# A sparse-attention and two-MoE kernel: later transposes of folded logits, ranks in portions, some local masks added by VectorE, last rows in separate tiles

## The chip, the core and the metric

The kernel runs on one core of a Trainium2 chip. A core has five engines with queues of their own, which meet only at semaphores: TensorE (PE, matrix products into PSUM; its weight loads are listed as PEld), VectorE (DVE), ScalarE (ACT), GpSimd (POOL) and SyncE (SP, which issues transfers). The metric is the device time of one execution in microseconds (us).

## The reference

```python
scores = scale * np.matmul(q, k.transpose(0, 1, 3, 2))          # batch 4, heads 8, seq 576, head_dim 64
mask_local = (rel >= 0) & (rel < 32)                            # heads 0 to 3
mask_strided = (rel >= 0) & (k_pos % 32 == q_pos % 32)          # heads 4 to 7
attn = softmax(np.where(masks, scores, -1e9)); x = attn @ v     # 2304 tokens x 512
h = np.maximum(x @ w_in, 0.0)                                   # d_ff 2048
x2 = (s * h * h + b) @ w_out
logits = x2 @ w_gate                                            # 8 experts
# all (token, expert) pairs by falling logit; a pair is taken if the token is free
# and the expert has fewer than 288 tokens
out[mask_e] = np.maximum(x2[mask_e] @ w1[e], 0.0) @ w2[e]       # per expert, F 1024
```

All data are fp32. The weights of the first layer pair come as 64-bit words, and the kernel converts them on chip.

## The kernel before, in words

**Products.** A matrix product in fp32 is made of three fp32r products: each operand is split into a rounded part and a rest (`xh`/`xl`, `wh`/`wl`, `u[:, 0]`/`u[:, 1]`), the rounded part by ScalarE, the rest by a subtraction on VectorE (L331, L350, L631).

**Stages.** Attention is cut into 32 units (`attn_unit`: a batch b, a pair of heads hp, a half hf). A unit writes a mask into PSUM by a bf16 matmul with the identity (L232), adds the scores of its blocks onto it (L239), and then VectorE takes the row maxima (L244), subtracts (L259), ScalarE takes the exponential, VectorE sums and scales (L264 to L267), PE transposes (L273) and multiplies with v (L294). Units with hp 0 and 1 are local: five blocks of 96 keys (hf 0, 480 columns) or four (hf 1, 384 columns). In batches 0 and 1 (b below `SEG` = 2) the exponential reads PSUM directly; batches 2 and 3 run between the matmuls of the hidden layer.

The tokens then go in six groups g of 384. `h_step(g, fc)` makes one of 16 slices of the hidden layer: twelve matmuls (L441), squared ReLU on ScalarE (L446, L447), and the slice goes to DRAM (`ud`). The logits come from the slices folded with `w_out @ w_gate` (L479): for groups 4 and 5 at once (`h_step`), for groups 0 to 3 (`DG`) later from DRAM (`fold_late`). `logits(g)` copies the folded sums from PSUM (ScalarE, L503), transposes them (PE, L507), reduces (VectorE, L512, L513), and when groups 0 to 3, or 4 and 5, are all there, `ranks` compares each expert pair of a token: seven steps of three operations (L525 to L527).

**The late layer.** x2 itself is made late: `late_step(g, fc)` loads a hidden slice back, splits it (L628 ScalarE, L631 VectorE) and queues nine matmuls (L658). `x2_late` hands them out one by one; they fill PE while other engines do the routing. `x2_row` (L496) scales a row tile and SyncE writes it to DRAM (`x2d`).

**Routing.** `route` runs seven rounds; a round finds each expert's threshold by four counts over 64 candidates (VectorE comparisons, PE sums L787 and L790), then a prefix over tokens (L694 to L700). At the end a last prefix, index arithmetic on VectorE (L798 to L825) and L830 make the list of tokens per expert (L834). Each yield of `route` carries a number of late matmuls to be put in.

**Experts.** `first_gather` fetches the first expert's rows by indirect transfers (GpSimd, L859), PE does the rest of the late layer beside it (L866); then each expert takes two layers (L912, L937). The last expert writes its rows in three parts (`put`, L980 to L982).

**Order.** The order on every engine is the order in which the program emits (`manual_schedule`). `Pipe.tick` advances all live generators by one `yield`; the loop of `mix1` emits, per step, folds (`FT` = 3 ticks), from n = 96 on `LF` = 3 late matmuls, and one tick of the pipe of `h_step`. A `yield` more in `logits` or `ranks` thus moves what follows it behind what others emit in that tick, and the loop ends only when all generators have ended.

Of the kernel before, what the change touches and what calls it, by code (L numbers as in the profile page):

```python
# [8 lines left out]
F32 = mybir.dt.float32  # L9
# [4 lines left out]
ALU = mybir.AluOpType  # L14
AX = mybir.AxisListType
# [47 lines left out]
class Body:  # L63
    B = 4
    H = 8
    S = 576
# [6 lines left out]
    NG = 6  # L73
    E = 8
    CAP = 288
# [62 lines left out]
    def constants(self):  # L138
# [26 lines left out]
        for h in (0, 64):  # L165
            nc.vector.tensor_copy(self.mstr[h:h + 36], t1[h:h + 36, :36].unsqueeze(1).to_broadcast([36, 8, 36]))
        self.Es = [c.tile([128, 8, 64], F32, name=f"E{i}") for i in range(self.NE)]
        for E in self.Es:
            nc.gpsimd.memset(E, 0.0)
        self.onesf = c.tile([128, 128], F32, name="onesf")  # L170
# [50 lines left out]
    def attn_unit(self, b, hp, hf):  # L221
        nc = self.nc
        loc = hp < 2
        p, nb, kw = (64, 5 - hf, 96) if loc else (36, 8, 36)
        pr = 64 + p
        qk, vs = self.load_unit(b, hp, hf)
        for _ in range(self.LOADLAG):
            yield
        sp = self.ps()
        m = self.mloc[:, hf:] if loc else self.mstr  # L230
        w = nb * kw
        nc.tensor.matmul(sp[:, :w], self.identb, m.rearrange("p c k -> p (c k)"),  # L232
                         start=True, stop=False, skip_group_check=True)
        for c in range(nb):
            q0 = c * p + 32 if loc and hf else c * p
            k0 = max(0, q0 - 32) if loc else q0
            for j in range(2):
                sl = slice(64 * j, 64 * j + 64)
                nc.tensor.matmul(sp[64 * j:64 * j + p, c * kw:(c + 1) * kw], qk[sl, 0, q0:q0 + p],  # L239
                                 qk[sl, 1, k0:k0 + kw], start=False, stop=(c == nb - 1), skip_group_check=True)  # L240
        yield
        nm = self.p2.tile([128, 2, 8], F32, tag="nm", name=self.nm("nm"), bufs=6)
        mx, sm = nm[:pr, 0, :nb], nm[:pr, 1, :nb]
        nc.vector.tensor_reduce(mx, sp[:pr, :w].rearrange("p (c k) -> p c k", c=nb), axis=AX.X, op=ALU.max, negate=True)  # L244
        if loc:
            E = self.wt([128, nb, kw], F32, "E")
        else:
            Ep = self.Es[self.ne % self.NE]
            self.ne += 1
            E = Ep[:, :, :36]  # L250
        if loc and b < self.SEG:
            nc.vector.tensor_scalar(mx, mx, 0.125, None, op0=ALU.mult)
            yield from self.lag(0, b)
            for c in range(nb):
                nc.scalar.activation(E[:pr, c, :], sp[:pr, c * kw:(c + 1) * kw], AF.Exp, bias=mx[:, c:c + 1],
                                     scale=0.125, accum_out=sm[:, c:c + 1])
            yield from self.lag(1, b)
        else:
            nc.vector.tensor_tensor(E[:pr], sp[:pr, :w].rearrange("p (c k) -> p c k", c=nb),  # L259
                                    mx.unsqueeze(2).to_broadcast([pr, nb, kw]), op=ALU.add)  # L260
            yield from self.lag(0, b)
            nc.scalar.activation(E[:pr], E[:pr], AF.Exp, scale=0.125)
            yield from self.lag(1, b)
            nc.vector.tensor_reduce(sm, E[:pr], axis=AX.X, op=ALU.add)  # L264
        nc.vector.tensor_scalar(sm, sm, 1e-9, None, op0=ALU.add)
        nc.vector.reciprocal(sm, sm)
        nc.vector.tensor_tensor(  # L267
            E[:pr], E[:pr], sm.unsqueeze(2).to_broadcast([pr, nb, kw]), op=ALU.mult)
        yield from self.lag(2, b)
        tps = [self.ps() for _ in range(2 if loc else 1)]  # L270
        for c in range(nb if loc else 4):
            if loc:
                nc.tensor.transpose(tps[c % 2][:96, 128 * (c // 2):128 * (c // 2) + 128], E[:, c, :], self.identf)  # L273
            else:
                nc.tensor.transpose(tps[0][:, 128 * c:128 * c + pr], Ep[:pr, 2 * c:2 * c + 2, :].rearrange("p m k -> p (m k)"),
                                    self.identf[:pr, :pr])
        yield
        eTs = []
        for t, tp in enumerate(tps):
            h, kr = ((nb - t + 1) // 2, 96) if loc else (4, 100)  # L280
            src = tp[:kr, :128 * h].rearrange("k (c j i) -> k c j i", j=2, i=64)[:, :, :, :p]
            eT = self.wt([128, h, 2, p], F32, "eT")
            (nc.vector.tensor_copy if (t and b > 1 if loc else self.TV) else nc.scalar.copy)(eT[:kr], src)
            eTs.append(eT)
        yield from self.lag(3, b)
        o = [self.ps() for _ in range(1 if loc else 2)]
        for c in range(nb):
            for j in range(2):
                if loc:
                    out, eT = o[0][64 * j:64 * j + 64, c * p:(c + 1) * p], eTs[c % 2][:96, c // 2, j, :]  # L290
                else:
                    m, k = c % 2, c // 2
                    out, eT = o[m][64 * j:64 * j + 64, k * p:(k + 1) * p], eTs[0][64 * m:64 * m + 36, k, j, :]
                nc.tensor.matmul(out, vs[c][:, j, :], eT, start=True, stop=True, skip_group_check=True)  # L294
        yield
        if b not in self.xb:
            self.xb[b] = self.xf.tile([128, 4, 576], F32, tag="xb", name=self.nm("xb"))
        if loc:
            nc.scalar.copy(self.xb[b][:, hp, 320 * hf:320 * hf + p * nb], o[0][:, :p * nb])
        else:  # L300
            dst = self.xb[b][:, hp, :].rearrange("d (i m c) -> d m c i", m=2, c=8)[:, :, 4 * hf:4 * hf + 4]
            for m in range(2):
                (nc.vector.tensor_copy if m and self.OV else nc.scalar.copy)(
                    dst[:, m], o[m][:, :144].rearrange("d (c i) -> d c i", c=4))
        self.units += 1
# [194 lines left out]
    def logits(self, g, pf):  # L500
        nc = self.nc
        fo = self.wt([128, self.G], F32, "fo")
        nc.scalar.copy(fo, pf[:, :self.G])  # L503
        yield
        ps = self.ps()
        for t in range(3):
            nc.tensor.transpose(ps[:, t * 128:(t + 1) * 128], fo[:, t * 128:(t + 1) * 128], self.identf)  # L507
        yield
        L = self.L[:, 3 * g:3 * g + 3, :]
        for t in range(3):  # L510
            v = ps[:, t * 128:(t + 1) * 128].rearrange("p (j k) -> p k j", j=4)[:, :8, :]
            nc.vector.tensor_reduce(L[:, t, :], v, axis=AX.X, op=ALU.add)  # L512
        nc.vector.scalar_tensor_tensor(L, L, self.sb[:, 0:1], self.lc.unsqueeze(1).to_broadcast([128, 3, 8]),  # L513
                                       op0=ALU.mult, op1=ALU.add)
        self.ranked.add(g)
        for gs in (range(4), range(4, 6)):
            if g in gs and self.ranked.issuperset(gs):
                self.ranks(3 * gs[0], 3 * gs[-1] + 3)

    def ranks(self, i, j):  # L520
        tt = self.nc.vector.tensor_tensor
        L, R = self.L[:, i:j, :], self.R[:, i:j, :]
        for d in range(1, 8):
            ge = self.ge[:, i:j, :8 - d]
            tt(ge, L[:, :, :8 - d], L[:, :, d:], op=ALU.is_ge)  # L525
            tt(R[:, :, :8 - d], R[:, :, :8 - d], ge, op=ALU.add)
            tt(R[:, :, d:], R[:, :, d:], ge, op=ALU.subtract)  # L527

    def mix1(self):
        nc = self.nc  # L530
# [436 lines left out]
    def last_expert(self, e, X, w1, w2):  # L967
        nc = self.nc
# [7 lines left out]
                                 start=(fc == 0 and i == 0), stop=(fc == 7 and i == 2))  # L976

        def put(c):
            t = self.wt([96, 512], F32, "yr")
            nc.scalar.copy(t[:, :256], y[c][:96, :256])  # L980
            nc.vector.tensor_copy(t[:, 256:], y[c][:96, 256:])
            nc.gpsimd.indirect_dma_start(  # L982
                out=self.a["out"][:, :],
                out_offset=bass.IndirectOffsetOnAxis(ap=self.idx[:, 3 * e + c:3 * e + c + 1], axis=0),
                in_=t, in_offset=None)
# [122 lines left out]
```

## Time and profile before

| | us |
|---|---|
| median of 3 runs | 823.06 |
| lowest, highest | 822.31, 823.54 |
| profiled execution | 822.38 |
| its span | 820.3 |
| PE busy (share of the span) | 798.2 (97%) |
| VectorE busy | 473.6 (58%) |
| ScalarE busy | 370.3 (45%) |

The mean granted clock of TensorE is 0.992 of full speed. A busy engine is not an engine at its peak: matmuls overlap, and their ends are modelled; the time from one start to the next is what a matmul costs, and the chain of waits counts so. In an idle entry such as `[2.15 <-DVE u L631]` the number is how long the engine stood still before the row, and behind the arrow is what ended it. A line number is that of the kernel before unless said otherwise.

### The profile page before, as it was taken

How to read it: one execution, taken by the hardware profiler on the slowest of the kernel's cores; microseconds unless marked ns; L12 is line 12 of the kernel's file. 1: busy time of each engine (PE TensorE's matmuls, PEld its weight loads, DVE VectorE, ACT ScalarE, POOL GpSimd, SP SyncE). 2: the span in 40 equal slices, each digit the busy share in tenths (PEclk: the TensorE clock that was granted, in tenths of full speed). 3: DMA queues.
4: the chain of work that ended last, by engine and by line, in shares of the span. 5: the costliest groups of instructions: out<-in, count | busy, mean ns of one | idle time of the engine just before them, and what ended most of it. 6: DMA issues, size and time to landing. Idle time of an engine off the chain costs nothing.

```text
span 820.3 us, 17310 instructions
## 1 busy us (share of the span) xinstructions
PE 798.2 (97%) x6688; PEld 697.9 (85%) x6688; DVE 473.6 (58%) x1160; ACT 370.3 (45%) x889; POOL 52.2 (6%) x69
## 2 busy tenths in 40 slices
PE   7989999999999999989999999999999999999996
PEld 5779988899999678877777777777899999999994
DVE  8798874667452234066676767565265556455620
ACT  3787665656564464422323222222245455445520
POOL 1000000000000000000000000000203112221211
PEclk9979999999999999999999999999999999999999
DMA  7958745746775894442516233332577566656410
GB/s 186 278 172 257 230 134 170 245 162 225 268 243 177 261 305 174 149 159 79 180 54 205 91 100 109 87 126 69 163 241 212 159 194 213 205 167 207 125 30 29
DMA packets 88753, 140.21 MB, mean 171 GB/s; under 512 B 10848, under 2 KB 52576, under 8 KB 88672
## 3 DMA queue, kind: packets, MB, share of 16 engines
q1 hardware_dynamic: 85600, 129.68, 50.2%
q0 software_dynamic: 3072, 9.44, 3.6%
q8 instruction: 52, 0.85, 0.4%
q14 instruction: 29, 0.24, 0.1%
HBM read 106.32 MB, written 32.77 MB: 170 GB/s over the span
## 4 chain that ended last, share of the span: by engine, by line
PE 92%; DVE 4%; ACT 1%; issue 1%; DMA 1%; POOLq 0%; POOL 0%; DVEq 0%; ACTq 0%; SPq 0%
PE b L441 26%; PE b L658 21%; PE b L912 12%; PE b L937 11%; PE b L239 3%; PE b L479 2%; PE b L787 2%; PE b L294 2%; PE b L397 2%; PE b L975 1%; PE b L866 1%; PE b L953 1%; PE b L390 1%; PE b L311 1%; PE b L273 1%
## 5 line engine op out<-in xcount | busy, mean ns | idle before, releaser
L658 PE MATMUL b<-wh,u 128*128 128x512 f32 x544 | 181.7, 404 | 2.6 <-DVE u L631 2.6
L658 PEld LDWEIGHTS b<-wh,u 128*128 128x128 f32 x544 | 101.6, 188 | 23.8 <-DVE u L631 3.8
L628 ACT CAST u<-r 128x384 fp32r<-128x384 f32 (+1 forms) x96 | 47.3, 496 | 161.8 <-PE b L658 127.0
L658 PE MATMUL b<-wl,u 128*128 128x512 f32 x272 | 106.8, 393 | 0.0
L937 PE MATMUL b<-u,wh 128*128 128x288 f32 x448 | 93.5, 302 | 0.0
L446 ACT ACTIVATE r<-b 128x384 f32<-128x384 f32 x96 | 47.1, 491 | 101.7 <-PE b L441 101.6
L441 PE MATMUL b<-xh,wh 128*128 128x384 f32 x384 | 89.9, 355 | 0.0
L350 DVE TENSOR_TENSOR wl<-raw,wh 128x512 fp32r<-128x512 f32 x128 | 82.9, 684 | 0.3
L441 PE MATMUL b<-xl,wh 128*128 128x384 f32 x384 | 83.0, 337 | 0.0
L441 PE MATMUL b<-xh,wl 128*128 128x384 f32 x384 | 82.8, 336 | 0.0
L912 PE MATMUL b<-X,wh 128*128 128x288 f32 x512 | 78.1, 295 | 0.6 <-ACT X L885 0.6
L348 ACT CAST wh<-raw 128x512 fp32r<-128x512 f32 x128 | 73.5, 620 | 4.0 <-DVE u L631 4.0
L441 PEld LDWEIGHTS b<-xh,wh 128*128 128x128 f32 x384 | 64.6, 190 | 12.1 <-issue 10.0
L912 PEld LDWEIGHTS b<-X,wh 128*128 128x128 f32 x512 | 71.5, 188 | 1.4 <-ACT X L885 0.7
L937 PEld LDWEIGHTS b<-u,wh 128*128 128x128 f32 x448 | 71.0, 188 | 0.0
L441 PEld LDWEIGHTS b<-xl,wh 128*128 128x128 f32 x384 | 69.0, 189 | 0.0
L441 PEld LDWEIGHTS b<-xh,wl 128*128 128x128 f32 x384 | 68.5, 189 | 0.0
L919 DVE SCALAR_TENSOR_TENSOR u<-b,u 128x288 fp32r<-128x288 f32 x64 | 29.1, 455 | 66.5 <-ACT u L918 66.5
L937 PE MATMUL b<-u,wl 128*128 128x288 f32 x224 | 65.9, 294 | 0.0
L631 DVE TENSOR_TENSOR u<-r,u 128x384 fp32r<-128x384 f32 (+1 forms) x96 | 48.9, 529 | 21.6 <-ACT u L628 21.6
L658 PEld LDWEIGHTS b<-wl,u 128*128 128x128 f32 x272 | 51.2, 188 | 9.3
L918 ACT ACTIVATE u<-b 128x288 fp32r<-128x288 f32 x64 | 26.4, 412 | 59.3 <-PE b L912 59.3
(201 smaller groups left out, 1164.0 us busy)
## 6 DMA issues: line engine op xcount, KB each, us to landing
raw<-in_moe_w_dram SPq DMA_DIRECT2D x128, 256.0 KB
r<-ud SPq DMA_DIRECT2D x160, 192.0 KB
ud<-r SPq DMA_DIRECT2D x96, 192.0 KB
raw<-in_words_dram SPq DMA_DIRECT2D x64, 256.0 KB
qk<-in_q_dram SPq DMA_DIRECT2D x24, 288.0 KB
x2d<-E SPq DMA_DIRECT2D x18, 256.0 KB
wod<-K SPq DMA_DIRECT2D x16, 256.0 KB
wo<-wod SPq DMA_DIRECT2D x16, 256.0 KB
```

The lines of the kernel that those rows point to most:

```text
L239: nc.tensor.matmul(sp[64 * j:64 * j + p, c * kw:(c + 1) * kw], qk[sl, 0, q0:q0 + p], qk[sl, 1, k0:k0 + kw], start=False, stop=(c == nb - 1 ...
L348: nc.scalar.copy(h, W)
L350: nc.vector.tensor_tensor(l, W, _f(h), op=ALU.subtract)
L441: nc.tensor.matmul(ps[:, :self.G], w[:, dc * 128:(dc + 1) * 128], self.xg[g][dc][x], start=(k == 0), stop=(k == 11))
L446: nc.scalar.activation(r, ps[:, :self.G], AF.Relu)
L628: nc.scalar.copy(d[:, 0, :], src)
L631: nc.vector.tensor_tensor(d[:, 1, :], src, _f(d[:, 0, :]), op=ALU.subtract)
L658: self.nc.tensor.matmul(**args)
L912: self.nc.tensor.matmul(ps[:, :288], w1[dc, fh][wi][:, fs:fs + 128], X[:, xi, dc, :], start=(k == 0), stop=(k == 11))
L918: self.nc.scalar.activation(h, ps[:, :288], AF.Relu)
L919: self.nc.vector.scalar_tensor_tensor(l, ps[:, :288], 0.0, _f(h), op0=ALU.max, op1=ALU.subtract)
L937: nc.tensor.matmul(y[dc][:, :288], w[:, sl], u[:, j, :288], start=(fc == 0 and i == 0), stop=(fc == 7 and i == 2))
```

## The change

1. Local units of batches 2 and 3 put no mask into PSUM. The first score matmul of a block starts it afresh, and VectorE adds the mask (`mloc`) while it copies the scores into E; the maxima and the subtraction then read E.
2. `logits` of groups 0 to 3 yields three times instead of once between the copy and the transposes.
3. `ranks` yields after each of its seven steps.
4. The last expert's rows go into the three tiles `Es`, not into tiles of the common pool.

```diff
--- before.py
+++ after.py
@@ -229,25 +229,31 @@
         sp = self.ps()
         m = self.mloc[:, hf:] if loc else self.mstr
         w = nb * kw
-        nc.tensor.matmul(sp[:, :w], self.identb, m.rearrange("p c k -> p (c k)"),
-                         start=True, stop=False, skip_group_check=True)
+        after = loc and b >= self.SEG
+        if not after:
+            nc.tensor.matmul(sp[:, :w], self.identb, m.rearrange("p c k -> p (c k)"),
+                             start=True, stop=False, skip_group_check=True)
         for c in range(nb):
             q0 = c * p + 32 if loc and hf else c * p
             k0 = max(0, q0 - 32) if loc else q0
             for j in range(2):
                 sl = slice(64 * j, 64 * j + 64)
                 nc.tensor.matmul(sp[64 * j:64 * j + p, c * kw:(c + 1) * kw], qk[sl, 0, q0:q0 + p],
-                                 qk[sl, 1, k0:k0 + kw], start=False, stop=(c == nb - 1), skip_group_check=True)
+                                 qk[sl, 1, k0:k0 + kw], start=after, stop=after or c == nb - 1, skip_group_check=True)
         yield
         nm = self.p2.tile([128, 2, 8], F32, tag="nm", name=self.nm("nm"), bufs=6)
         mx, sm = nm[:pr, 0, :nb], nm[:pr, 1, :nb]
-        nc.vector.tensor_reduce(mx, sp[:pr, :w].rearrange("p (c k) -> p c k", c=nb), axis=AX.X, op=ALU.max, negate=True)
         if loc:
             E = self.wt([128, nb, kw], F32, "E")
         else:
             Ep = self.Es[self.ne % self.NE]
             self.ne += 1
             E = Ep[:, :, :36]
+        S = sp[:pr, :w].rearrange("p (c k) -> p c k", c=nb)
+        if after:
+            nc.vector.tensor_tensor(E, S, m, op=ALU.add)
+            S = E
+        nc.vector.tensor_reduce(mx, S, axis=AX.X, op=ALU.max, negate=True)
         if loc and b < self.SEG:
             nc.vector.tensor_scalar(mx, mx, 0.125, None, op0=ALU.mult)
             yield from self.lag(0, b)
@@ -256,8 +262,7 @@
                                      scale=0.125, accum_out=sm[:, c:c + 1])
             yield from self.lag(1, b)
         else:
-            nc.vector.tensor_tensor(E[:pr], sp[:pr, :w].rearrange("p (c k) -> p c k", c=nb),
-                                    mx.unsqueeze(2).to_broadcast([pr, nb, kw]), op=ALU.add)
+            nc.vector.tensor_tensor(E[:pr], S, mx.unsqueeze(2).to_broadcast([pr, nb, kw]), op=ALU.add)
             yield from self.lag(0, b)
             nc.scalar.activation(E[:pr], E[:pr], AF.Exp, scale=0.125)
             yield from self.lag(1, b)
@@ -501,7 +506,8 @@
         nc = self.nc
         fo = self.wt([128, self.G], F32, "fo")
         nc.scalar.copy(fo, pf[:, :self.G])
-        yield
+        for _ in range(1 if g > 3 else self.FT):
+            yield
         ps = self.ps()
         for t in range(3):
             nc.tensor.transpose(ps[:, t * 128:(t + 1) * 128], fo[:, t * 128:(t + 1) * 128], self.identf)
@@ -515,7 +521,7 @@
         self.ranked.add(g)
         for gs in (range(4), range(4, 6)):
             if g in gs and self.ranked.issuperset(gs):
-                self.ranks(3 * gs[0], 3 * gs[-1] + 3)
+                yield from self.ranks(3 * gs[0], 3 * gs[-1] + 3)
 
     def ranks(self, i, j):
         tt = self.nc.vector.tensor_tensor
@@ -525,6 +531,7 @@
             tt(ge, L[:, :, :8 - d], L[:, :, d:], op=ALU.is_ge)
             tt(R[:, :, :8 - d], R[:, :, :8 - d], ge, op=ALU.add)
             tt(R[:, :, d:], R[:, :, d:], ge, op=ALU.subtract)
+            yield
 
     def mix1(self):
         nc = self.nc
@@ -976,7 +983,7 @@
                                  start=(fc == 0 and i == 0), stop=(fc == 7 and i == 2))
 
         def put(c):
-            t = self.wt([96, 512], F32, "yr")
+            t = self.Es[c].rearrange("p c k -> p (c k)")[:96]
             nc.scalar.copy(t[:, :256], y[c][:96, :256])
             nc.vector.tensor_copy(t[:, 256:], y[c][:96, 256:])
             nc.gpsimd.indirect_dma_start(
```

In the changed kernel line numbers are a few higher: L441 becomes L446, L479 L484, L503 L508, L507 L513, L525 to L527 L531 to L533, L631 L638, L658 L665, L694 L701, L798 L805, L830 L837.

**PE at the logits of group 0.** `b_3268` holds the folded sums, `fo_4127` their copy, `b_4131` (now `b_4158`) the transposes; `xh`, `xl`, `wh` belong to the hidden layer. Before:

```order
L479 MATMUL b_3268<-r_4042,wog 32x384
L479 MATMUL b_3268<-r_4095,wog 32x384
L507 MATMUL b_4131<-identf,fo_4127 128x128 x3
L441 MATMUL b_4153<-xh_3743,wh_1632 128x384
L441 MATMUL b_4153<-xh_3776,wh_1632 128x384
L441 MATMUL b_4153<-xh_3820,wh_1632 128x384
L441 MATMUL b_4153<-xh_3853,wh_1632 128x384
```

In the changed kernel (the four L484 of `b_3268` and the first four L446 of `b_4145` stand right above):

```order
L446 MATMUL b_4145<-xl_3744,wh_1631 128x384
L446 MATMUL b_4145<-xl_3777,wh_1631 128x384
L446 MATMUL b_4145<-xl_3821,wh_1631 128x384
L446 MATMUL b_4145<-xl_3854,wh_1631 128x384
L446 MATMUL b_4145<-xh_3743,wl_1632 128x384
L446 MATMUL b_4145<-xh_3776,wl_1632 128x384
L446 MATMUL b_4145<-xh_3820,wl_1632 128x384
L446 MATMUL b_4145<-xh_3853,wl_1632 128x384
L513 MATMUL b_4158<-identf,fo_4127 128x128 x3
L484 MATMUL b_3317<-r_4097,wog 32x384
L484 MATMUL b_3317<-r_4099,wog 32x384
```

The transposes have moved behind the twelve matmuls of one slice of the hidden layer. For groups 1 and 3 it is the same; for 2, 4 and 5 their place is unchanged.

**VectorE at a local unit of batch 2.** `b_1869` are the scores, `nm` the maxima. Before:

```order
L267 TENSOR_TENSOR E_113<-E_113,nm_1739 100x8x36
L244 TENSOR_REDUCE nm_1946<-b_1869 128x5
L259 TENSOR_TENSOR E_1948<-b_1869,nm_1946 128x480
L283 COPY eT_1971<-b_1935 96x256
L350 TENSOR_TENSOR wl_1904<-K_1726,wh_1903 128x512
```

In the changed kernel:

```order
L272 TENSOR_TENSOR E_113<-E_113,nm_1739 100x8x36
L254 TENSOR_TENSOR E_1946<-b_1869,mloc 128x480
L256 TENSOR_REDUCE nm_1945<-E_1946 128x5
L265 TENSOR_TENSOR E_1946<-E_1946,nm_1945 128x480
L288 COPY eT_1971<-b_1934 96x256
L355 TENSOR_TENSOR wl_1903<-K_1726,wh_1902 128x512
```

One operation more (L254), which reads PSUM; the other two read and write E. On PE the L232 that stood ahead of the L239 of `b_1869` is gone with its weight load: PE has 5481 rows for 5497, VectorE 1125 for 1117.

**VectorE at the ranks of groups 4 and 5.** `ge` and `R` are the comparisons and ranks, `u` the late splits. Before, the end of the 21 operations:

```order
L527 TENSOR_TENSOR R<-R,ge 128x6x2
L525 TENSOR_TENSOR ge<-L 128x6
L526 TENSOR_TENSOR R<-R,ge 128x6
L527 TENSOR_TENSOR R<-R,ge 128x6
L631 TENSOR_TENSOR u_4863<-r_4834,u_4863 128x384
L631 TENSOR_TENSOR u_4908<-r_4842,u_4908 128x384
L631 TENSOR_TENSOR u_4922<-r_4865,u_4922 128x384
L631 TENSOR_TENSOR u_4936<-r_4910,u_4936 128x384
```

In the changed kernel, from the third operation on:

```order
L533 TENSOR_TENSOR R<-R,ge 128x6x7
L638 TENSOR_TENSOR u_4863<-r_4834,u_4863 128x384
L531 TENSOR_TENSOR ge<-L 128x6x6
L532 TENSOR_TENSOR R<-R,ge 128x6x6
L533 TENSOR_TENSOR R<-R,ge 128x6x6
L531 TENSOR_TENSOR ge<-L 128x6x5
L532 TENSOR_TENSOR R<-R,ge 128x6x5
L533 TENSOR_TENSOR R<-R,ge 128x6x5
L531 TENSOR_TENSOR ge<-L 128x6x4
L532 TENSOR_TENSOR R<-R,ge 128x6x4
L533 TENSOR_TENSOR R<-R,ge 128x6x4
L638 TENSOR_TENSOR u_4890<-r_4842,u_4890 128x384
```

The first late split now stands behind three operations, the second behind twelve, the next four behind all 21. On PE 58 matmuls of the late layer instead of 37 stand between the last transposes of logits and the first of the routing, and 28 instead of 49 between L830 and L866.

## Rows read from the trace of the kernel before

**Rows 1.** The profile's page: busy time of each engine, and shares of the chain

```profile
PE 798.2 (97%) x6688; PEld 697.9 (85%) x6688; DVE 473.6 (58%) x1160; ACT 370.3 (45%) x889; POOL 52.2 (6%) x69
...
PE 92%; DVE 4%; ACT 1%; issue 1%; DMA 1%; POOLq 0%; POOL 0%; DVEq 0%; ACTq 0%; SPq 0%
```

**Rows 2.** What PE waited for, whole span (us in total, times, longest)

```profile
PE b L658 <- DVE u L631: 2.6, 3, 2.1
...
PE b L507 <- ACT fo L503: 2.0, 3, 0.7
...
PE b L694 <- DVE rt L766: 0.7, 1, 0.7
PE b L830 <- DVE rt L824: 0.6, 1, 0.6
...
PE b L830 <- DVE rt L825: 0.3, 1, 0.3
```

**Rows 3.** The chain (start us, us, what), 88 to 182 us

```profile
89.15 0.22 PE b L232
...
113.49 0.18 PE b L232
...
166.41 0.16 PE b L232
```

**Rows 4.** VectorE's groups, 88 to 182 us (busy us, mean ns | idle)

```profile
L267 DVE TENSOR_TENSOR E<-E,nm 128x480 f32<-128x480 f32 x4 | 2.6, 658 | 0.1
L259 DVE TENSOR_TENSOR E<-b,nm 128x480 f32<-128x480 f32 x4 | 2.6, 658 | 0.1
...
L331 DVE TENSOR_TENSOR xl<-xb,xh 128x384 fp32r<-128x384 f32 x4 | 2.2, 559 | 6.4 <-ACT xh L330 6.4
L259 DVE TENSOR_TENSOR E<-b,nm 128x384 f32<-128x384 f32 x4 | 2.2, 558 | 0.1
```

**Rows 5.** Busy time by engine, nine stretches from 88 to 182 us together

```profile
sum 94.00, PE 94.00 PEld 84.66 DVE 64.45 ACT 57.53 POOL 0.00; mean PE 10.44 PEld 9.41 DVE 7.16 ACT 6.39 POOL 0.00
```

**Rows 6.** Time line (start us, us, what [idle before <-releaser]), 144 us

```profile
144.65 0.56 DVE L331 TENSOR_TENSOR xl<-xb,xh 128x384 fp32r<-128x384 f32 x1 [0.35 <-ACT xh L330]
...
144.85 0.85 PE L441 MATMUL b<-xl,wh 128*128 128x384 f32 x4
```

**Rows 7.** The chain: logits, one late step, the late matmuls behind the routing

```profile
277.17 0.49 ACT fo L503
...
277.71 0.55 PE b L507 x3
...
300.51 0.33 PE b L507 x3
...
343.20 2.09 PE b L658 x9
...
562.95 11.27 PE b L658 x49
```

**Rows 8.** Time line, VectorE and PE, 348 to 354 us

```profile
348.75 0.20 DVE L525 TENSOR_TENSOR ge<-L 128x42 f32<-128x42 f32 x1
...
352.75 1.96 DVE L631 TENSOR_TENSOR u<-r,u 128x384 fp32r<-128x384 f32 x4
...
353.35 0.73 PE L658 MATMUL b<-wh,u 128*128 128x512 f32 x2 [2.15 <-DVE u L631]
```

**Rows 9.** Time line, VectorE and PE, 549 to 552 us

```profile
550.97 0.43 DVE L631 TENSOR_TENSOR u<-r,u 128x256 fp32r<-128x256 f32 x1 [0.90 <-ACT u L628]
...
551.51 0.16 DVE L798 TENSOR_SCALAR rt<-b 128x8 f32<-128x8 f32 x1
...
549.92 0.23 PE L700 MATMUL b<-gsb,onesb 128*128 128x152 bf16 x1
```

**Rows 10.** Time line of VectorE and GpSimd (POOL), indices and first gather

```profile
562.99 0.18 DVE L834 CAST idx<-b 96x24 int32<-96x24 f32 x1 [1.25 <-PE b L830]
...
578.18 1.08 POOL L859 DMA_INDIRECT xr<-x2d,idx  x1 [372.16 <-PE b L866]
```

## Prediction

> **What bounds the kernel now.** I read the page first. Its first section has TensorE (PE) busy for 97% of the span, VectorE (DVE) for 58%, ScalarE (ACT) for 45%; its fourth gives PE 92% of the chain that ended last, DVE 4%, ACT 1% [rows 1]. The reader is to see that PE sets the time almost throughout, so that an edit is worth what it takes off PE or off a wait of PE. The second view is therefore PE's waits over the whole span [rows 2]: they are few and short, 2.6 us for the split L631, 2.0 us for the folded logits' copy L503, 0.7 us and 0.6 + 0.3 us for routing steps. After that I read, place by place, the chain where the masks and the logits stand [rows 3, 7], VectorE's durations there [rows 4], the engines' busy time [rows 5], and time lines at the places where PE could begin to wait [rows 6, 8 to 10]. The granted clock is no term: in the masks' stretch the row has PE busy for 94.00 of 94.00 us, and the change leaves no new gap there by my forecast [rows 5].
>
> **The change, part by part.** The sum is made against the profiled execution, 822.38 us (span 820.3 and 2.08 around it). The median of the three runs is 823.06, 0.68 above it; I add these 0.68 at the end.
>
> *Masks of batches 2 and 3.* Removed are eight mask matmuls, four of 480 columns and four of 384. On the chain the former are pieces of 0.22 us (four alike), the latter two of 0.18 and two of 0.16 [rows 3]: 4 x 0.22 + 2 x 0.18 + 2 x 0.16 = 1.56 us of PE. A piece runs from start to start, so weight loads that did not hide are in it. The trace has no such addition on VectorE; the nearest row is the subtraction L259 of the same shape, also from PSUM to SBUF, 658 and 558 ns [rows 4]. So VectorE gets 4 x 0.658 + 4 x 0.558 = 4.86 us more. What hides that: in 94 us VectorE is busy 64.45, so nearly 30 us are free [rows 5]. The tight spot is the fifth unit, the first of batch 3: behind its L259 stands the split L331 of token group 2 at 144.65, and PE's first four xl matmuls run from 144.85 in 0.85 us, the last of them on this split [rows 6]. L331 there waited 0.35 us for ScalarE's xh, so an addition of 0.66 in front of it makes it 0.3 us later, of which PE may feel 0 to 0.3. If the cover were gone everywhere, PE would wait 4.86 and gain 1.56: +3.3. Bounds -1.56 to +3.3; I take -1.5, near the chain's pieces, since L331 waits for ScalarE in all four cases here (6.4 us) [rows 4].
>
> The Trainium skill, "TensorE: Matmul & The Clock Gate", section "Back-to-back issue gap", speaks against the size: it gives a sustained spacing of about 131 ns for 512 columns. By that the eight would be worth an estimated 1.0 us, and the sum would be 0.5 us smaller; the pieces of 0.22 us for 480 columns [rows 3] don't agree, and I go by them. "Perfetto Trace Analysis" of the Trainium skill, section "Optimizing Scalar/DVE Operations", gives VectorE about 60 ns of overhead on SBUF and 125 on PSUM; by it the reduction and the subtraction, which now read SBUF, would give back an estimated 16 x 0.065 = 1.0 us of VectorE's time. The trace disagrees: the same shape takes 658 ns from PSUM (L259) and 658 from SBUF (L267) [rows 4], and nothing is given back.
>
> *Transposes of the folded logits.* Before, three times PE ends the fold, waits for the copy L503 and only then transposes: from the copy's start at 277.17 to the end of L507 at 277.71 + 0.55 it is 1.09 us; where the copy had long been done L507 takes 0.33 [rows 7]. That is 0.76 at most each time; the waits themselves add up to 2.0 [rows 2]. The order on PE now has twelve matmuls of a hidden layer between fold and transposes for groups 0, 1 and 3. The copy needs 0.49 us and of those matmuls four take 0.85 [rows 6], twelve over 2; ScalarE's order around it is as before. Bounds 2.0 to 2.3, I take 2.1; it isn't below nothing, since the copy stands where it stood and PE does the same work. Behind it the ranks of groups 0 to 3 come later, but no PE instruction waits for them until the routing.
>
> *Ranks in portions.* At 348.75 VectorE starts 21 small operations, and four late splits L631 stand behind them from 352.75; PE stands still for 2.15 us until 353.35 [rows 8]. PE had run dry 2.15 us earlier, at 351.2. Now a split stands after the first three rank operations, the next after twelve, the others after all 21. Three operations take (352.75 - 348.75) x 3/21 = 0.57 us, so the first split, of 1.96/4 = 0.49 us, ends at about 349.8, 1.4 us ahead of the need. Twelve take 2.29: the second ends at 352.0. A late step is nine matmuls (three row tiles by three products) in 2.09 us [rows 7], so PE needs it at 351.2 + 2.1 = 353.3. The third ends at 348.75 + 4.0 + 3 x 0.49 = 354.2, against 355.4. ScalarE's casts are no limit: the four splits ran without a gap [rows 8]. Gain 2.15; bounds 1.1 (half of it comes back at the second split) and 2.15; it isn't below nothing, since VectorE does the same operations and PE has more to do beside them. The seven extra steps of the loop carry 3 late matmuls each, 21 in all, from behind the routing to in front of it; their sum is the same. Cover given up: behind the routing 28 stay of 49, where 49 take 11.27 us [rows 7], so 21 x 0.23 = 4.8 us less hide the way from the indices to the gathers. The indices are there at 562.99, the first gather starts at 578.18 [rows 10]: 15 us apart, and the gather waits for the last rows of x2, which move along with the late matmuls. Cost 0.
>
> *End of the routing.* The shift by 21 matmuls puts other splits beside the last routing steps. Before, VectorE's L798 stands behind a split at 550.97 that itself waited 0.90 for ScalarE; it starts at 551.51, though PE had its operand by 549.92 + 0.23 [rows 9]; so the L694 behind it waits 0.7, and the L830 0.6 + 0.3 [rows 2]. In the new order the splits ahead of it are of older steps whose casts are done, and I expect L798 straight behind PE. Bounds 0 and 1.6 (all three gone); I take 1.1.
>
> *Last rows in tiles of their own.* The three scatters wait for the same semaphores as before, and each tile is still written by the same copies of ScalarE and VectorE, one behind the other. Worth 0.
>
> Sum: 1.5 + 2.1 + 2.15 + 1.1 = 6.85; 822.38 - 6.85 = 815.5, with 0.68 added 816.2 us.
>
> **The rivals.**
> *New small waits* (R1). The late matmuls now meet other VectorE work than before: a row tile's x2 or a routing step in front of a split. For it: two of the three L658 waits before are of this kind, (2.6 - 2.1)/2 = 0.25 each [rows 2]. Against: they are only two in some 200 us. Ten of them would cost 2.5: 816.2 + 2.5 = 818.7.
> *VectorE's additions come late* (R2). The mask additions stand in front of splits on which the next matmuls rest, at every unit and not only at 144.65; PE then loses 4.86 and gains 1.56. For it: the narrow margin at 144.85 [rows 6]. Against: 30 free us [rows 5]. 816.2 + 4.86 = 821.1.
> *Routing hand-overs* (R3, the other side). Place: the seven routing rounds, each with four counts, four sums of them and a prefix that PE takes over from VectorE, 63 hand-overs. If with the shift the splits, themselves late as at 550.97, stand in front of the routing step at many of them, each costs what L694 waits, 0.7 [rows 2, 9]. It decides from (6.85 + 1.65)/0.7 = 12.1, 13 of the 63 on; with 14 it is 9.8 us: 816.2 + 9.8 = 826.0. For it: the one row of this kind that exists. Against: before it is one of 63.
> *A part does nothing*: the last tiles, as said, by identical waits; that is in the forecast.
>
> **How the numbers follow.** The forecast has 0.68, R1 0.15, R2 0.10, R3 0.07. The forecast's own range: all upper bounds (1.56 + 2.3 + 2.15 + 1.6 = 7.6) give 815.5, 1.0 below for what I don't see: 814.5; the lower ones (1.2 + 2.0 + 1.1 + 0) give 818.8. The range reaches over R1 to 820.0; outside stay R3, most of R2 and a few per cent below. A measurement of this kernel tells 0.2%, 1.65 us, from no change: faster is below 821.4, slower above 824.7. Faster: 0.68 + 0.14 of R1 + 0.05 of R2 = 0.87; same: 0.01 + 0.05 + 0.03 of R3 = 0.09; slower: 0.04.
>
> **What would show it.** In the changed profile's list of PE's waits the row for the logits' copy is gone and that of L631 (now L638) has only the two short ones; L694's and L830's (now L701, L837) shrink. PE has eight mask matmuls fewer, with 1.5 us less PE time between 88 and 182 us and eight new VectorE operations of 0.56 to 0.66. The forecast is wrong in a part if its wait stays or comes back under another name within the next few us: at the first xl matmuls of group 2 for the masks, behind the twelve matmuls for the logits, at the second late step for the ranks, and at the routing's matmuls for the shift.

## The result: 815.11 us, and the profile after

The changed kernel takes 815.11 us (814.41 to 815.69, 4 runs), the kernel before 823.3 in the same comparison (822.31 to 825.18, 4 runs): ratio 0.9898, 95% interval 0.9884 to 0.9912. Two more comparisons gave 0.9903 and 0.9906. The forecast was 816.2. The profiled execution of after took 815.69 (span 813.9), 6.7 less than the one of before; the medians stand 8.2 apart. Why the two differ is the main thing to explain below.

From the page of the changed kernel, busy times and shares of the chain:

```profile
PE 796.1 (98%) x6680; PEld 697.4 (86%) x6680; DVE 477.6 (59%) x1168; ACT 370.3 (45%) x889; POOL 51.8 (6%) x69
...
PE 93%; DVE 4%; ACT 1%; issue 1%; DMA 0%; POOLq 0%; POOL 0%; DVEq 0%
```

PE's share of the chain rose from 92 to 93% [rows 1]; VectorE has 4.0 us more. What PE waited for, whole span (us in total, times, longest):

```profile
...
PE b L299 <- ACT eT L288: 2.1, 3, 1.0
PE b L665 <- DVE u L638: 2.1, 4, 0.8
...
PE b L919 <- ACT X L892: 0.6, 1, 0.6
```

Against [rows 2]: the logits' copy (2.0) is gone, so are the routing's end (0.7, 0.6, 0.3) and the 2.1 us at the ranks. But the late splits (L638 is the L631 of before) still cost 2.1 us, now in four pieces.

**Masks.** Time line of PE at two fixed places, one ahead of the first local unit of batch 2 and one behind the last of batch 3: first in a kernel that has the masks of before (experiment tail_only), then in the changed one.

```profile
81.96 0.30 PE L232 MATMUL b<-mstr,identb 128*128 128x288 bf16 x1
...
271.07 1.02 PE L424 MATMUL b<-acc,onesf 128*128 128x512 f32 x2
```

```profile
83.45 0.30 PE L234 MATMUL b<-mstr,identb 128*128 128x288 bf16 x1
...
271.08 1.02 PE L429 MATMUL b<-acc,onesf 128*128 128x512 f32 x2
```

From mark to mark 189.11 us before, 187.63 after: 1.48 us less, where the sum had 1.5 [rows 3]; the profile of the kernel before has the same 189.11 (83.78 to 272.89). The first mark itself lay between 81.8 and 83.8 us in the profiles of one and the same start, so stages are compared between these two marks, called the first and the second mark below, or from a mark to the end of the span, and not by their place in the span. A part of that spread is the clock: in every profile it falls once more ahead of the first mark, at some 45 to 60 us, in eight of them with 3.4 us lost and in five with 5.1, and the first mark lies at 82.1 us on average in the eight and at 83.0 in the five.

**Logits.** The chain at group 0 (start us, us, what):

```profile
274.43 0.78 PE b L484 x8
275.22 2.31 PE b L446 x12
277.53 0.33 PE b L513 x3
```

The transposes take 0.33 us, as where nothing was waited for [rows 7], and stand right behind the hidden layer's matmuls.

**Ranks.** Time line of VectorE (start us, us, line, operation):

```profile
344.49 0.20 DVE L531 TENSOR_TENSOR ge<-L 128x42 f32<-128x42 f32 x1
...
345.08 0.55 DVE L638 TENSOR_TENSOR u<-r,u 128x384 fp32r<-128x384 f32 x1
...
347.33 0.55 DVE L638 TENSOR_TENSOR u<-r,u 128x384 fp32r<-128x384 f32 x1
...
349.18 1.49 DVE L638 TENSOR_TENSOR u<-r,u 128x384 fp32r<-128x384 f32 x3
```

The first split starts 0.59 us after the first rank operation, the second 2.84 after it, three more in a row behind all 21. PE stood still for 2.15 us at this place [rows 8] and now has no wait. What that is worth from start to start is read from the last transposes of logits to the first prefix of the routing, in the kernel before (the last row is the seventh prefix, of use further on) and in phase_back, which has the same number of late matmuls between the two (time line of PE):

```profile
347.52 0.49 PE L507 MATMUL b<-identf,fo 128*128 128x128 f32 x3
...
386.95 0.24 PE L694 MATMUL b<-rt,ltri 128*128 128x144 bf16 x1
...
549.17 0.24 PE L694 MATMUL b<-rt,ltri 128*128 128x144 bf16 x1
```

```profile
342.44 0.49 PE L513 MATMUL b<-identf,fo 128*128 128x128 f32 x3
...
379.40 0.24 PE L701 MATMUL b<-rt,ltri 128*128 128x144 bf16 x1
```

39.43 us before, 36.96 after: 2.47 less. A listed wait counts from the modelled end of the matmul ahead of it, and this one is 0.3 us shorter than what it cost.

**Routing.** Time line of VectorE, then of PE, in one of the seven rounds:

```profile
412.86 0.17 DVE L805 TENSOR_SCALAR rt<-b 128x8 f32<-128x8 f32 x1 [0.72 <-PE b L707]
...
416.01 1.36 DVE L788 TENSOR_TENSOR rt<-rt,cand 128x1152 bf16<-128x1152 f32 x1
417.28 2.06 DVE L501 SCALAR_TENSOR_TENSOR E<-b,sb,acc 128x512 f32<-128x512 f32 x3
419.26 1.02 DVE L638 TENSOR_TENSOR u<-r,u 128x384 fp32r<-128x384 f32 x2
...
418.64 0.39 PE L665 MATMUL b<-wl,u 128*128 128x512 f32 x1
419.86 0.49 PE L665 MATMUL b<-wh,u 128*128 128x512 f32 x1 [0.83 <-DVE u L638]
```

Here stands a new wait. From 412.86 to 417.37 VectorE makes twelve routing operations up to the comparison L788, then three x2 rows (L501), and only then the split for which PE has waited 0.83 us. The same happens once more 82 us later, and twice without the x2 rows (0.21). From start to start these waits too cost more than is listed; the prefix of the first, second, third and seventh round (from after_third, the changed kernel again):

```profile
384.00 0.24 PE L701 MATMUL b<-rt,ltri 128*128 128x144 bf16 x1
...
410.86 0.24 PE L701 MATMUL b<-rt,ltri 128*128 128x144 bf16 x1
...
438.83 0.24 PE L701 MATMUL b<-rt,ltri 128*128 128x144 bf16 x1
...
548.54 0.24 PE L701 MATMUL b<-rt,ltri 128*128 128x144 bf16 x1
```

A round without such a wait takes 26.86 us, the one with the wait listed at 0.8 takes 27.97: 1.11 more. From the first prefix to the seventh it is 164.54 us here and 162.22 in the kernel before (386.95 to 549.17), so the rounds have become 2.3 us longer. And at the routing's end, VectorE, then PE:

```profile
550.55 0.17 DVE L805 TENSOR_SCALAR rt<-b 128x8 f32<-128x8 f32 x1
...
550.29 0.23 PE L707 MATMUL b<-gsb,onesb 128*128 128x152 bf16 x1
...
553.17 0.24 PE L701 MATMUL b<-rt,ltri 128*128 128x144 bf16 x1
```

L805 starts as soon as L707 is through (550.29 + 0.23), and L701 starts without a wait. Before, the same operation came 1.4 us after PE [rows 9].

### The profile page after: what moved, and what is told of

It reads as the page before. It is cut to its first block, busy times and chain, and to the rows that moved or that the text cites. A ratio compares the mean times of both kernels' runs of the same rounds, so it can differ in the third digit from the quotient of the medians.

```text
span 813.9 us, 17313 instructions
## 1 busy us (share of the span) xinstructions
PE 796.1 (98%) x6680; PEld 697.4 (86%) x6680; DVE 477.6 (59%) x1168; ACT 370.3 (45%) x889; POOL 51.8 (6%) x69
## 4 chain that ended last, share of the span: by engine, by line
PE 93%; DVE 4%; ACT 1%; issue 1%; DMA 0%; POOLq 0%; POOL 0%; DVEq 0%
PE b L446 26%; PE b L665 22%; PE b L919 13%; PE b L944 11%; PE b L241 3%; PE b L794 2%; PE b L484 2%; PE b L299 2%; PE b L402 2%; PE b L982 1%; PE b L873 1%; PE b L960 1%; PE b L395 1%; PE b L316 1%; PE b L278 1%
## 5 line engine op out<-in xcount | busy, mean ns | idle before, releaser
L665 PE MATMUL b<-wh,u 128*128 128x512 f32 x544 | 181.9, 404 | 2.1 <-DVE u L638 2.1
L665 PEld LDWEIGHTS b<-wh,u 128*128 128x128 f32 x544 | 101.5, 188 | 24.0 <-DVE u L638 4.1
L665 PE MATMUL b<-wl,u 128*128 128x512 f32 x272 | 106.8, 393 | 0.0
L446 PE MATMUL b<-xh,wh 128*128 128x384 f32 x384 | 90.0, 356 | 0.0
L446 PE MATMUL b<-xl,wh 128*128 128x384 f32 x384 | 83.0, 337 | 0.0
L446 PE MATMUL b<-xh,wl 128*128 128x384 f32 x384 | 82.6, 336 | 0.0
L919 PE MATMUL b<-X,wh 128*128 128x288 f32 x512 | 78.1, 295 | 0.6 <-ACT X L892 0.6
L446 PEld LDWEIGHTS b<-xh,wh 128*128 128x128 f32 x384 | 64.4, 190 | 13.4 <-issue 11.3
L919 PEld LDWEIGHTS b<-X,wh 128*128 128x128 f32 x512 | 71.5, 188 | 1.4 <-ACT X L892 0.7
L446 PEld LDWEIGHTS b<-xl,wh 128*128 128x128 f32 x384 | 69.0, 189 | 0.0
L446 PEld LDWEIGHTS b<-xh,wl 128*128 128x128 f32 x384 | 68.5, 189 | 0.0
L638 DVE TENSOR_TENSOR u<-r,u 128x384 fp32r<-128x384 f32 (+1 forms) x96 | 49.0, 528 | 18.3 <-ACT u L635 18.2
L665 PEld LDWEIGHTS b<-wl,u 128*128 128x128 f32 x272 | 51.2, 188 | 9.2
```

Source lines behind the costliest of these rows:

```text
L446: nc.tensor.matmul(ps[:, :self.G], w[:, dc * 128:(dc + 1) * 128], self.xg[g][dc][x], start=(k == 0), stop=(k == 11))
L638: nc.vector.tensor_tensor(d[:, 1, :], src, _f(d[:, 0, :]), op=ALU.subtract)
L665: self.nc.tensor.matmul(**args)
L919: self.nc.tensor.matmul(ps[:, :288], w1[dc, fh][wi][:, fs:fs + 128], X[:, xi, dc, :], start=(k == 0), stop=(k == 11))
```

## The experiments

**Each part alone.** Every kernel is the one before with one of the four parts of the change.

*masks_only*. 

> Only the masks of batches 2 and 3 are changed. Theory: eight PE pieces of 1.56 us in all go, VectorE's 4.86 us more are hidden; 1.5 us faster than before (ratio 0.9982), PE's other waits as before. Rival (VectorE's additions come late): PE waits at first xl matmuls or weight splits, up to +3.3 us, ratio up to 1.004.

Measured 822.34 us, ratio 0.9992 (0.9980 to 1.0004): not told from no change, and less than expected. Between the marks its profile has the same 187.63 us as the changed kernel's, so the 1.48 us are won there. In this execution they are lost again further on; busy time by stretch of 3 us (PE busy, PEld, VectorE, ScalarE, POOL, PEclk, DMA share, GB/s):

```profile
349.00:352.00 3.00, 1.61 (x4) 1.32 (x5) 2.90 (x12) 0.00 (x0) 0.00 (x0) 0.73 0.89 266
352.00:355.00 3.00, 3.00 (x11) 2.42 (x10) 0.95 (x3) 0.51 (x1) 0.00 (x0) 0.70 1.06 388
```

PEclk is the granted clock as a share of full speed. PE stands still here for 2.15 us, as in [rows 8], and right behind it the granted clock falls to its lower level (1.2 instead of 2.4 GHz) for a part of two stretches: 3 x (0.27 + 0.30) = 1.71 us lost. The same execution shows it once more behind the routing's end. From the second mark to the end it takes 550.5 us, 3.1 more than the profile of the kernel before (547.4), for 3.4 us lost at the lower clock. In the profile of the kernel before neither place shows it (the same columns):

```profile
340.00:360.00 20.00, 17.85 (x89) 13.82 (x87) 9.72 (x38) 7.01 (x15) 0.00 (x0) 1.00 0.78 256
555.00:575.00 20.00, 19.01 (x113) 15.75 (x112) 11.98 (x35) 5.36 (x18) 0.00 (x0) 1.00 0.27 80
```

That most of the eleven runs lost as much is not shown; only this one has a trace.

*logits_only*. 

> Only the logits of groups 0 to 3 yield three times before their transposes. Theory: PE's wait for the copy L503 (2.0 us in three) is gone, 2.1 us faster than before, ratio 0.9975. Rival: the wait comes back at another instruction behind the twelve matmuls or at the ranks, ratio 1.000.

Measured 820.46 us, ratio 0.9973 (0.9960 to 0.9985), 2.2 us: as expected in the time. The rival has a share in the profile, though: all three waits for the copy are gone, but from the second mark to the last transposes it is only 1.4 us shorter than the kernel before, and PE's weight loads at the folds (L479) now wait for hidden slices from DRAM (`r`), 1.3 us in four. The profile of the changed kernel has 0.5 in two of these.

*ranks_only*. 

> Only the ranks yield after each step. Theory: PE's wait of 2.15 us for the late split is gone; by the shift of 21 late matmuls the waits at the routing's end (1.67 us) go too, but the four waits of 2.1 us in the rounds come that the changed kernel shows, so that the shift by itself is worth 0.0: 2.2 us faster, ratio 0.9973. Rival (the routing's end is a gain of its own): 3.3 us faster, ratio 0.9960.

Measured 818.97 us, ratio 0.9951 (0.9937 to 0.9965): 4.0 us by the ratio, 3.7 between the medians, nearer to the rival's number and beyond both. But its waits are those that the theory named, and not the rival's:

```profile
PE b L659 <- DVE u L632: 2.1, 4, 0.8
```

So the waits of the late layer and the routing add up to 2.1 us instead of 4.2. From the first mark to the end its profile takes 734.2 us, that of the kernel before 736.5: 2.3 less, as the theory had it, and neither execution has the lower clock in there but in its last few us. The rest of the 4.0 is therefore not in these two profiles; the runs of before that fall to the lower clock are the candidate.

*tail_only*. 

> Only the last expert's rows go into tiles of their own. Theory: the same waits, so 0.0 us, ratio 1.000. Rival: the third scatter no longer waits for a buffer, and the end comes up to 0.3 us earlier, ratio 0.9996.

Measured 823.09 us, ratio 1.0003 (0.9994 to 1.0012): nothing, as expected. Its profile (the same columns as above) shows the lower clock behind the routing's end, where PE had waited 0.7, 0.6 and 0.3 us:

```profile
558.00:561.00 3.00, 2.05 (x38) 1.77 (x37) 1.91 (x6) 0.00 (x0) 0.00 (x0) 1.00 0.03 7
561.00:564.00 3.00, 3.00 (x12) 2.40 (x11) 1.79 (x7) 0.63 (x3) 0.00 (x0) 0.59 0.53 154
564.00:567.00 3.00, 3.00 (x12) 2.40 (x12) 1.25 (x4) 1.18 (x4) 0.00 (x0) 0.84 0.31 104
```

Lost are 3 x (0.41 + 0.16) = 1.71 us, the same as above; from the second mark to the end it takes 548.9 us, 1.5 more than the profile of before. This made the theory that the next four kernels test: a standstill of PE of some 2 us costs itself, and in many executions 1.7 us more at the lower clock behind it.

**after_again**, the changed kernel itself. 

> The changed kernel once more, beside the others. Expected 815.1 us, ratio 0.9898 as before; PE's waits 2.1 us for L638 in the routing rounds, none at the logits, the ranks and the routing's end. Theory (a standstill of PE of about 2 us is followed in many executions by a stretch at the lower clock that costs about 1.7 us more): the granted clock is 1.00 in 340 to 360 us and 555 to 575 us in every profile of it. Rival (the clock falls there by chance): it shows 0.91 there as often as the kernels that kept the standstills.

Measured 814.79 us, ratio 0.9903 (0.9888 to 0.9918). The two stretches in the first profile of the changed kernel:

```profile
340.00:360.00 20.00, 20.00 (x95) 15.42 (x94) 11.06 (x48) 5.98 (x13) 0.00 (x0) 1.00 0.56 185
555.00:575.00 20.00, 19.98 (x118) 16.70 (x117) 9.31 (x25) 3.04 (x10) 2.55 (x3) 1.00 0.21 69
```

PEclk is 1.00 in both places; so it is in all three profiles of the changed kernel and in ranks_only's, which has neither standstill either.

**fill_waits**, the kernel before with useless matmuls where PE stands still:

```diff
                 self.ranks(3 * gs[0], 3 * gs[-1] + 3)
+                if g > 3:
+                    self.keep_warm(14)
...
+        self.keep_warm(4)
         yield self.FE[0]
...
+        self.keep_warm(6)
         yield self.FE[2]
```

> The kernel before, with 14 useless matmuls of 288 columns (about 2 us) on PE right behind the last logits' transposes, where PE later stands still for 2.15 us, and 4 and 6 of them ahead of the two waits at the routing's end. They fill standstills and save no wait. Theory of the lower clock: 0.5 to 2 us faster than before, ratio 0.9978 to 0.9994, and the granted clock 1.00 in 340 to 360 and 555 to 575 us. Rival (the standstill alone costs): 0.0 to 0.3 us slower, ratio 1.000 to 1.0004.

Measured 821.71 us, ratio 0.9980 (0.9971 to 0.9989): 1.6 us faster, though nothing but work was added. In its profile the span from the first mark on is 736.8 us, against 736.5 in that of the kernel before (820.3 - 83.8), which had no lower clock at these places: so the filling by itself saves no time, and neither of these two executions can show the gain. It shows in the runs: 0.9971 to 0.9989 leaves out the rival's 1.000 to 1.0004. The clock in both stretches:

```profile
340.00:360.00 20.00, 19.61 (x102) 14.99 (x101) 10.17 (x41) 7.02 (x15) 0.00 (x0) 1.00 0.75 247
555.00:575.00 20.00, 19.66 (x118) 16.22 (x117) 12.01 (x35) 4.75 (x16) 0.00 (x0) 1.00 0.25 78
```

**phase_back**, the changed kernel without the shift of 21 late matmuls:

```diff
-    LATE0 = 30
+    LATE0 = 9
```

> The changed kernel with 9 instead of 30 late matmuls ahead of the routing, which takes back the shift by 21. Theory: the waits at the routing's end (0.7 + 0.6 + 0.3) come back and the four waits of 2.1 shrink to 0.4, so the waits add up to the same; the lower clock behind the routing's end comes back in part of the executions, so 0 to 1.7 us slower than the changed kernel, ratio 0.990 to 0.992. Rival (the shift was a gain of its own): 1.6 us or more slower in every execution, with no change of the four waits.

Measured 816.78 us, ratio 0.9923 (0.9910 to 0.9937), 2.0 us slower than after_again on the same chip, a little beyond the expected 0 to 1.7. The waits did as the theory said and not as the rival did; the four waits shrank:

```profile
PE b L701 <- DVE rt L773: 0.7, 1, 0.7
PE b L837 <- DVE rt L831: 0.7, 1, 0.7
...
PE b L665 <- DVE u L638: 0.4, 2, 0.2
...
PE b L837 <- DVE rt L832: 0.3, 1, 0.3
```

They add up to 2.1 us, as in the changed kernel. Behind them its profile has the lower clock, 3 x (0.47 + 0.10) = 1.71 us:

```profile
555.00:558.00 3.00, 3.00 (x17) 2.52 (x16) 1.78 (x7) 0.60 (x2) 0.00 (x0) 0.53 0.44 117
558.00:561.00 3.00, 3.00 (x13) 2.37 (x13) 1.01 (x4) 1.21 (x4) 0.00 (x0) 0.90 0.43 145
```

From the second mark to the end it takes 544.5 us, the three profiles of the changed kernel 542.6 to 542.8: the difference is that one fall, and in waits the shift by itself is worth nothing.

**split_early**, the changed kernel with the late splits one step earlier:

```diff
             nc.vector.tensor_tensor(d[:, 1, :], src, _f(d[:, 0, :]), op=ALU.subtract)
         yield
+        yield
```

> The changed kernel, with one yield more in late_step between the late split and its matmuls, so that VectorE makes each split one late step (2.05 us) earlier. Theory (the four waits for L638, 0.8 + 0.2 + 0.8 + 0.2 us, are splits that stand behind thirteen routing operations and three x2 rows): all four go, 2.1 us faster than the changed kernel, ratio 0.987 to the kernel before. Rival (VectorE is short of time there and the wait moves to a routing step): no change to the changed kernel, ratio 0.990.

Measured 816.42 us, ratio 0.9917 (0.9904 to 0.9931): 1.6 us slower than after_again. All four waits are gone, but a split that waits for its cast now stands in front of the last index arithmetic, and PE waits at L838 (the L830 of before):

```profile
PE b L838 <- DVE rt L832: 1.3, 1, 1.3
...
PE b L838 <- DVE rt L833: 0.3, 1, 0.3
```

Behind it the clock falls (1.71 us again):

```profile
555.00:558.00 3.00, 1.35 (x21) 1.01 (x20) 2.96 (x8) 0.60 (x2) 0.00 (x0) 1.00 0.00 0
558.00:561.00 3.00, 3.00 (x27) 2.54 (x26) 0.96 (x5) 0.23 (x1) 0.00 (x0) 0.65 0.00 0
561.00:564.00 3.00, 3.00 (x12) 2.42 (x11) 0.63 (x2) 0.38 (x2) 0.00 (x0) 0.78 0.02 5
```

So the rival had the outcome, but not for its reason. From the second mark to the end this profile takes 542.9 us with 1.71 lost at the lower clock, the changed kernel 542.6 to 542.8 without: the waits alone save about 1.6 us, and the clock takes them back. The profiled execution (814.82) is one of the two fastest of five; what the others, at 816.4 to 817.0, lose beyond it has no trace.

**split_early_fe**, the same with more late matmuls ahead of L838, beside the changed kernel (**after_third**):

```diff
-    FE = (4, 14, 10)
+    FE = (4, 14, 20)
```

> The changed kernel a third time, so that split_early_fe stands beside it on the same chip. Expected 814.9 us, ratio 0.990.

> The changed kernel with the late splits one step earlier, as in split_early, and with 20 instead of 10 late matmuls (2.3 us more) between the last index arithmetic and L838, where split_early got a new wait of 1.6 us and the lower clock behind it. Theory: no wait of PE is left between the routing's begin and L838, and no lower clock behind it; 2.1 us faster than the changed kernel, 812.8 us, ratio 0.9877. Rival (the wait moves on, to the gathers or to L838 again, or the lower clock comes anyway): as split_early or the changed kernel, 0.990 to 0.992.

Measured 814.73 us for after_third (ratio 0.9906, 0.9891 to 0.9921) and 812.55 for split_early_fe (0.9880, 0.9865 to 0.9895). All of its four runs (811.64 to 813.61) lie below all of after_third's (814.66 to 815.66): it beats both kernels, by 10.4 and 2.2 us. Of the waits in the routing one of 0.80 us is left, ahead of L838, where the theory had none:

```profile
556.80 0.74 PE L666 MATMUL b<-wh,u 128*128 128x512 f32 x2 [0.80 <-DVE u L638]
```

No lower clock follows it in this profile. The listed waits fall by 1.3 us only (2.1 to 0.8), but from start to start each of its rounds takes the 26.86 us of a round without a wait, and from the second mark to the end it is 2.4 us shorter than after_third (540.4 for 542.8).

**masks_twice**, the changed kernel with the mask added twice:

```diff
             nc.vector.tensor_tensor(E, S, m, op=ALU.add)
+            nc.vector.tensor_tensor(E, S, m, op=ALU.add)
```

> The changed kernel with VectorE's mask addition made twice in each of the eight units (the second writes the same numbers again), 4.86 us more of VectorE's time between 84 and 173 us. Theory (the addition is hidden): as the changed kernel, at most 0.5 us slower by PE's wait at the first xl matmuls of group 2; ratio 0.990 to 0.991. Rival (VectorE's additions come late): 2 to 4.9 us slower than the changed kernel, ratio 0.993 to 0.996.

Measured 815.17 us, ratio 0.9909 (0.9896 to 0.9923): the same as after_third. Between the marks it takes 188.04 us, 0.41 more than the changed kernel for 4.86 more on VectorE. At the place that the forecast called tight, PE's first xl matmuls run from 142.05 to 142.90, and the split ends at 143.54:

```profile
142.05 0.85 PE L447 MATMUL b<-xl,wh 128*128 128x384 f32 x4
...
142.99 0.55 DVE L337 TENSOR_TENSOR xl<-xb,xh 128x384 fp32r<-128x384 f32 x1
```

They do not rest on it, then: the forecast read that row wrongly, and the place was not tight.

## Why the prediction was right, and what it sized wrongly

The time lies in the range, 1.1 us from the forecast. By its steps:

- **Masks**: 1.5 forecast, 1.48 between the marks. Right, though masks_only as a whole (0.7 us) could not tell it from nothing; that VectorE's 4.86 us are hidden is shown by masks_twice, where another 4.86 cost 0.41. The place named for the risk was wrong. Of what was weighed there, the rows' 0.22 us per matmul came out, and not the estimate of 1.0 us for all eight from the Trainium skill's "TensorE: Matmul & The Clock Gate", section "Back-to-back issue gap".
- **Logits**: 2.1 forecast; 2.0 us of waits gone, 2.2 us by logits_only, and 2.1 from the second mark to the last transposes (74.63 us before, 72.54 in phase_back). Right.
- **Ranks**: the wait of 2.15 us is gone with the splits about where the forecast put them (the second ends at 347.33 + 0.55, 3.4 after the first rank operation; forecast 3.25). Right as a wait; as a size 2.15 was taken for the most that it could be, and from start to start it is 2.47. The shift's cost behind the routing, 0 forecast, is 0: PE's one listed wait behind the gathers (L912, now L919) is 0.6 us in both.
- **End of the routing**: 1.1 forecast. The waits there did go, 0.7 + 0.6 + 0.3, and more than was forecast. But rival R1 came at the same time and by the same shift: the four splits behind routing steps and x2 rows wait 2.1 us where before two of these were 0.4 to 0.5 together. From start to start the rounds take 2.3 us more, and from the seventh prefix to L830 it is 2.1 less (549.17 to 561.25 before, 548.54 to 558.50 in after_third). The net is 0.0, shown by phase_back, where both change back and the waits add up to the same. The forecast gave the two a choice; they are two faces of one shift.
- **The granted clock**: "is no term" was the mis-sized step. It was read from the masks' stretch only and from one execution of before, which happened to have 1.00 at both later standstills. Behind such standstills the clock falls in a part of the executions: at the ranks in one profile of four (before, masks_only, logits_only, tail_only), behind the routing's end in four of six (these and phase_back, split_early), each time with 1.71 us lost. In six profiles of kernels with neither standstill (the changed kernel three times, ranks_only, masks_twice, split_early_fe) it never did at these two places.
- **Last rows**: 0.0 forecast, 0.0 by tail_only.

The sum of waits and work is therefore 1.5 + 2.1 + 2.5 + 0.0, some 6 us, and that much the profiles show: from the first mark to the end 736.5 us before and 730.3 to 730.5 in the three of the changed kernel, none of them with a fall behind the first mark other than at the very end. The medians differ by 8.2. That the other 2 us are the lower clock, which the median run of before pays for, is supported but not fully shown: an estimate from the profiles is 1.71 x (1/4 + 4/6) = 1.6 us, fill_waits, which takes away only the standstills, won 1.6, and 0.3 to 0.5 stay open. How often a run of before falls was not counted in more than these profiles. The mean clock that is known of every run does not count it either: it is 0.9914 over 46 runs of before and 0.9923 over 12 of the changed kernel, which by itself would be some 0.7 us, and masks_only has runs of 818.6 and 823.6 us at the same 0.990.

That the forecast came out so near is luck in part: the 1.1 of the routing's end, which did not come, was made up by the lower clock, which it left out.

## What to carry to other kernels

A standstill of TensorE can cost more than is listed for it. From start to start a wait listed at 0.8 us cost 1.1 here, and behind standstills of 1.6 to 2.2 us in all the clock fell in five of ten cases: look at the granted clock in the few microseconds behind one, in more than one execution, and try filling it with work even if the work is useless (fill_waits won 1.6 us). The Trainium skill, "Perfetto Trace Analysis", section "Matmul Optimizations", says that the engine's power follows its use and that matmuls should come back to back; the falls behind the standstills here, 1.71 us each, agree. A shift of filler work removes the waits at one place and can make as many at another, so list all waits of the shifted stretch in both orders before a gain is booked. Where a wait is a split behind a burst on an in-order engine, making the split one step earlier can work, if what it then stands in front of has slack of its own: split_early did not have it, split_early_fe did.

## What was not expected of the hardware

Each fall of the clock at these standstills cost the same 1.71 us (four profiles, five falls, PEclk 0.53 to 0.90 in two neighbouring stretches of 3 us), behind a standstill of 2.15 us as behind waits of 1.6 in all. It did not come every time: tail_only, which up to there is the program of before, had it behind the routing's end, and the profile of before had not. One long wait is not needed: the fall at some 45 to 60 us, in all thirteen profiles, stands where PE's single waits are at most 1.2 us (in before 0.36 and 1.14 us in the 3 us ahead of it). Why it cost 3.4 us in eight profiles and 5.1 in five, the changed kernel's three among them, no run shows.
